# A packed attention and two MLP layers on one core: input splits made in pairs, conversions of w_in2 spread from step 46

## The chip, the cores and the metric

The kernel runs on one core of a Trainium2 chip. The time is the device time of one launch in microseconds (us), the median of several runs. The engines of the core work side by side and wait for one another by semaphores: TensorE (PE; its weight loads are listed as PEld), VectorE (DVE), ScalarE (ACT), GpSimd (POOL), and SyncE (SP), which here issues all DMA transfers in the order of the program. Every engine does its own instructions in order. The kernel fixes that order by hand.

## The reference

Eight batches of eight heads; 576 tokens, head size 64, 32 packed rows. With x the attention's output as 4608 rows of 512:

```
p_packed = softmax(p k^T / 8) v ;  a = softmax(q p_packed^T / 8) p_packed
x (4608 x 512) = a, heads side by side
h1 = x @ w_in1 (512 x 2048);  g1 = max(0.01 h1, h1);   y   = g1 @ w_out1 (2048 x 512)
h2 = y @ w_in2 (512 x 2048);  g2 = h2 * sigmoid(1.702 h2);  out = g2 @ w_out2 (2048 x 512)
```

The weights come as float64 words and are made float32 on the chip ("conversion").

## The kernel before

There are four stages. The first does attention and the product with w_in1 together and writes g1 to memory (g1_scratch, feature by token). The second, **y**, is g1 @ w_out1. The third, **h**, is y @ w_in2 with the gated activation and writes g2. The fourth, **sum**, is g2 @ w_out2. y, h and sum multiply by a scheme of seven products in place of eight for a two-by-two split of the matrices (tokens in halves i of 384, features in halves h), so their inputs need sums first. Each product is done to nearly full float32 precision with three matmuls on split inputs: an operand is a rounded high part and a remainder, and high x high, high x low and low x high are added.

y and sum have the same plan, `prepare`. The tokens are cut into 6 blocks of 768; a block has 7 products of 8 steps (`steps`: block, product p in the order 1, 7, 5, 6, 2, 4, 3, and f from 0 to 7), 56 steps in all. A step takes one 128-feature slice of an input of 384 tokens. In y it has six matmuls (L649), in sum nine (L761). Before step k, `high` (L489 and on) makes the split input: ScalarE copies 128x384 to the rounded high part (L491), and one step later VectorE subtracts it from the source to get the low part (in `split`, L107; every split of the kernel has this line). The two parts lie in a ring of ROLL = 5 slots; the copy for step k is emitted at step k - 3, the subtraction at k - 2. The copy must wait until TensorE has finished with the slot's last user, step k - 5.

The sources are `raws`, tiles of two features by 384 tokens (128x768) for the four quarters (token half, feature half), each loaded for the next block when the last reader of this one is done. Four series of sums, each of four VectorE instructions of 128x768, change them in place: S3 (L479) before product 7, S1 (L481) before product 5, S2 (L483) before product 6, S4 (L485) before product 3. After S4 the quarter (0,0) of the next block is loaded. When a product ends, `evacuate` adds or copies its bank: by ScalarE after products 1, 7 and 2 (L510, L512, L516), by VectorE after 5, 6, 4 and 3 (L514, L519, L524), with one more sum (L520) three steps after product 6 and the stores of c11, v, c10, c01.

The order is an agenda: `at(step, todo)` puts work on a step, and `side(step)` emits it ahead of that step's matmuls. `pieces` puts the parts of a generator on given steps. `combined` does so for the conversions: each of the 16 pieces of w_in2 loads its raw words at step s (L138, L139, on SP); from s + late on come ScalarE's two instructions (L121, L122), a step later VectorE's mask (L125), a step later its shift (L128) and GpSimd's add (L129), three steps on two subtractions (L144, L145), then two more (L147, L148), and the store of the seven combinations, wi_scratch (L151). The tiles raw, v and b of a conversion exist once, so the next must wait for their last use. These sixteen conversions lie among y's steps.

`y_block` makes the inputs of h the same way, for a block of y: it loads four quarters (L578), splits each of the seven products' inputs in two halves (`one`, L585 and L107), and makes sums in place between them (L591 to L596). That of block 0 lies in the last block of y, that of block 1 at h's start, and the later ones in h. Weights for h are split by `new_weights` (L625 and L107), those for sum in halves on sum's first steps (L458 and L107).

Of the kernel before, what the change touches and what calls it, by code (L numbers as in the profile page):

```python
# [9 lines left out]
F32 = mybir.dt.float32  # L10
F32R = mybir.dt.float32r
# [10 lines left out]
P = 128  # L22
# [4 lines left out]
HB = TB // 2  # L27
# [12 lines left out]
PLACE = {1: (0, 0), 7: (0, 0), 5: (1, 0), 6: (0, 0), 2: (0, 1), 4: (1, 1), 3: (0, 1)}  # L40

COMBO = {1: 0, 2: 1, 3: 2, 5: 3, 7: 4, 6: 5, 4: 6}
EARLY = 5
ROLL, LEAD = 5, 2


def packed_attention_moe_moe_kernel(tc, qT, kT, vm, vt, pT, w_in1, w_out1, w_in2, w_out2, out):
# [4 lines left out]
    nc = tc.nc  # L52
# [13 lines left out]
    pools = {}  # L66
# [13 lines left out]
    with ExitStack() as ctx:  # L80
# [10 lines left out]
        def at(step, *todo):  # L91
            agenda.setdefault(step, []).extend(todo)
# [9 lines left out]
        def split(step, high):  # L102


            rest = []
            at(step, lambda: rest.extend(high()))
            at(step + 1, lambda: nc.vector.tensor_sub(*rest))  # L107

        def pieces(piece, steps):

            for step in steps:
                at(step, lambda: next(piece, None))
# [19 lines left out]
        def combine(name, source, scratch):  # L132


            conv = pools["conv"]
            raw = conv.tile([P, 4, 256], U32, tag="raw", name=f"raw_{name}")
            for i, (x, y) in enumerate(((0, 1), (0, 0))):
                nc.sync.dma_start(raw[:, i], source[:, x, y])  # L138
            nc.sync.dma_start(raw[:, 2:4], source[:, 1])  # L139
            yield  # L140
            b = conv.tile([P, 8, P], F32, tag="b", name=f"b_{name}")
            v = conv.tile([P, 4 * P], F32, tag="v", name=f"v_{name}")
            yield from to_f32(b[:, 0:4].rearrange("p i w -> p (i w)"), raw.rearrange("p i (w t) -> p (i w) t", t=2), v, True)
            nc.vector.tensor_sub(b[:, 4], b[:, 0], b[:, 1])  # L144
            nc.vector.tensor_sub(b[:, 5], b[:, 3], b[:, 0])  # L145
            yield
            nc.vector.tensor_sub(b[:, 6], b[:, 3], b[:, 4])  # L147
            nc.vector.tensor_sub(b[:, 7], b[:, 2], b[:, 6])  # L148
            if scratch is not wo1c:
                yield  # L150
                nc.sync.dma_start(place(name, scratch), b[:, 1:8])  # L151
                return
            yield
            h = pools["px"].tile([P, 2, 7, P], F32R, tag="hl", name=f"hl_{name}")
            nc.scalar.copy(h[:, 0], b[:, 1:8])
            yield
            nc.vector.tensor_sub(h[:, 1], b[:, 1:8], h[:, 0].bitcast(F32))
            yield
            for x in range(2):
                nc.sync.dma_start(place(name, scratch)[:, x], h[:, x].bitcast(F32))  # L160
# [5 lines left out]
        def combined(what, first, late):  # L166

            view, to = {"wo1": (w_out1_v, wo1c), "wi2": (w_in2_v, wi2c), "wo2": (w_out2_v, wo2c)}[what]
            for n, s in enumerate(first):
                j, u = divmod(n, 2)  # L170
                src = view[:, :, u, :, j, :] if what == "wi2" else view[:, :, j, :, u, :]
                pieces(combine(f"{what}_{j}_{u}", src, to), (s, *(s + late + k for k in (0, 1, 2, 5, 6, 7, 8, 9))))
# [232 lines left out]
        for n in range(4, 16):  # L405
            s = 5 * (n // 4) - 5 + n % 4
# [6 lines left out]
        for b in range(B):  # L413
            s = 32 * b
# [18 lines left out]
        wt, raws, ga, outs, early = {}, {}, {}, {}, {}  # L433
# [29 lines left out]
        def load_raw(blk, i, h, fp, nm, g):  # L463
            if blk < NBK:
                home, tag = "dr", f"r{i}{h}{fp}"
                if nm == "d":
                    home, tag = ("cy", f"y{fp}") if (i, h) == (1, 0) else ("d" if h else "d0", tag)
                t = pools[home].tile([P, 2, HB], F32, tag=tag, name=f"{nm}r_{blk}_{i}{h}{fp}")
                f0, t0 = NJ * h + 2 * fp, TB * blk + HB * i
                nc.sync.dma_start(t, g[f0:f0 + 2, :, t0:t0 + HB].rearrange("f p t -> p f t"))  # L470
                raws[blk, i, h, fp] = t

        def prepare(nm, g):


            def combo(blk, fp, what):
                a11, a12, a21, a22 = (raws.get((blk, i, h, fp)) for i in range(2) for h in range(2))
                if what == "S3":
                    nc.vector.tensor_sub(a11, a11, a21)  # L479
                elif what == "S1":  # L480
                    nc.vector.tensor_add(a21, a21, a22)  # L481
                elif what == "S2":
                    nc.vector.tensor_sub(a11, a22, a11)  # L483
                else:
                    nc.vector.tensor_sub(a12, a12, a11)  # L485
                    load_raw(blk + 1, 0, 0, fp, nm, g)

            def high(k, blk, p, f):
                src = raws[(blk, *PLACE[p], f // 2)][:, f % 2, :]  # L489
                t = ga[blk, p, f] = pools["dr"].tile([P, 2, HB], F32R, tag=f"s{k % ROLL}", name=f"{nm}a_{blk}_{p}_{f}")  # L490
                nc.scalar.copy(t[:, 0, :], src)  # L491
                return t[:, 1, :], src, t[:, 0, :].bitcast(F32)

            for blk in range(NBK):
                s = 7 * NJ * blk
                for what, when in (("S3", (1, 4, 7, 10)), ("S1", (12, 14, 16, 19)), ("S2", (20, 22, 24, 27)), ("S4", (34, 38, 42, 46))):
                    for fp, k in enumerate(when):
                        at(s + k, lambda blk=blk, fp=fp, what=what: combo(blk, fp, what))
            for k, step in enumerate(steps):
                split(k - LEAD - 1, lambda k=k, step=step: high(k, *step))  # L500
                blk, p, f = step
                if f % 2 and p in (5, 4, 3):
                    at(k - LEAD, lambda blk=blk, p=p, f=f: load_raw(blk + 1, *PLACE[p], f // 2, nm, g))

        def evacuate(k, blk, p, bank, shape, store):
            def tile_(what):
# [31 lines left out]
        for k in range(EARLY):  # L538
            s = 32 * (B - 2) + 20 + 8 * k
# [29 lines left out]
        def y_block(early, steps, blk):  # L569

            t0 = TB * blk
            q = {}

            def load():
                for i, j in ((0, 0), (1, 0), (1, 1), (0, 1)):
                    home, tag = ("dr", f"r10{2 * i + j}") if blk == 0 else ("cy", f"y{2 * i + j}")
                    q[i, j] = pools[home].tile([P, 2, HB], F32, tag=tag, name=f"yq_{blk}_{i}{j}")
                    nc.sync.dma_start(q[i, j], yT[2 * j:2 * j + 2, :, t0 + HB * i:t0 + HB * i + HB].rearrange("d p t -> p d t"))  # L578

            def one(p, k):  # L580
                src, i = q[PLACE[p]], PRODUCTS.index(p)
                if blk not in ya:
                    ya[blk] = pools["ABC"[blk % 3]].tile([P, 7, 2, 2, HB], F32R, tag="ABC"[blk % 3], name=f"ya_{blk}")
                t = ya[blk][:, i]
                nc.scalar.copy(t[:, 0, k], src[:, k])  # L585
                return t[:, 1, k], src[:, k], t[:, 0, k].bitcast(F32)

            def combo(p):
                sub = nc.vector.tensor_sub
                if p == 1:  # L590
                    sub(q[0, 0], q[0, 0], q[1, 0])  # L591
                    nc.vector.tensor_add(q[1, 0], q[1, 0], q[1, 1])
                elif p == 7:
                    sub(q[0, 0], q[1, 1], q[0, 0])
                elif p == 6:
                    sub(q[0, 1], q[0, 1], q[0, 0])  # L596
            at(early, load)
            for n, step in enumerate(steps):
                p, k = (1, 2, 7, 5, 6, 4, 3)[n // 2], n % 2
                split(step, lambda p=p, k=k: one(p, k))  # L600
                if k:
                    at(step + 1, lambda p=p: combo(p))

        PIECES = (slice(0, 2), slice(2, 4), slice(4, 6), slice(6, 7))
# [27 lines left out]
        first_raws("b", g1)  # L632
        later_weights(lambda n: "w5" if n < 8 else "d", wo1c, "wo1")
        prepare("b", g1)
        combined("wi2", [26, 44] + [56 * blk + k for blk in range(1, 5) for k in (1, 19, 38)] + [281, 299], 14)
        last = 7 * NJ * (NBK - 1)
        y_block(last + 24, range(last + 28, last + 56, 2), 0)
        side_until(0)
        for k, (blk, p, f) in enumerate(steps):
# [82 lines left out]
        for q in range(2):  # L722
            s = 14 * NJ * q
# [3 lines left out]
        for k in range(EARLY):  # L727
            s = 7 * (4 * NJ + 2 * k + 2)
# [22 lines left out]
        first_raws("d", g2)  # L751
        later_weights(lambda n: "d", wo2c, "wo2")
        prepare("d", g2)
        side_until(0)
        for k, (blk, p, f) in enumerate(steps):
# [55 lines left out]
```

## Time and profile before

| | before |
|---|---|
| runs | 1472.9, 1468.38, 1469.59 us, median 1469.59 |
| the profiled execution | 1471.63 us; its span, first to last instruction, 1469.8 us |
| TensorE busy | 1403.5 us |
| VectorE, ScalarE, GpSimd busy | 1106.6, 836.6, 100.0 us |
| mean granted TensorE clock | 0.989 of full speed |
| y, from its first matmul to h's first | 352.4 to 734.3 us |
| sum, first to last matmul | 1100.5 to 1465.2 us |

A line of the profile names the place in the kernel (L649), the engine, the operation, and the tiles written and read. Tile names: br and ba are the raw and split inputs of y, dr and da those of sum, yq and ya those of h; wo and wj are weights; raw_wi, v_wi and b_wi are the tiles of a conversion of w_in2. A step of y can be told from the time, since a step's matmuls follow each other without gaps unless an engine is late.

### The profile page before, as it was taken

What the parts mean: (1) busy time and instruction counts of PE and PEld (TensorE: products, weight loads), DVE (VectorE), ACT (ScalarE), POOL (GpSimd) and SP (SyncE); (2) the same over time, 40 slices, a digit from 0 to 9 for tenths busy, and PEclk for the clock granted to TensorE, in tenths of its full rate; (3) what the DMA queues carried; (4) which work ended last, traced back from release to release, by engine and by line L of the source; (5) the groups of instructions that cost most, each with busy time, mean ns of one, the idle gap of its engine ahead of it and who ended that gap; (6) DMA issues with size and microseconds to landing.
All of it is one profiled execution on the core that took longest, in us unless ns stands there. A gap on an engine that the chain in (4) does not pass through costs nothing.

```text
span 1469.8 us, 27704 instructions
## 1 busy us (share of the span) xinstructions
PE 1403.5 (95%) x10400; PEld 1315.9 (90%) x10400; DVE 1106.6 (75%) x2068; ACT 836.6 (57%) x1791; POOL 100.0 (7%) x71
## 2 busy tenths in 40 slices
PE   6899999998999999999899999999999999999998
PEld 4577777778899999999789999999999999999998
DVE  6757677753688878888878787887558887787776
ACT  4666666755454555545566666666545555445443
POOL 1401110100011011010100000100000000000000
PEclk7999999999999999999999999999999999999999
DMA  9679999979965563655267777777667534515421
GB/s 340 227 259 331 315 315 328 298 244 340 355 205 183 179 220 98 215 180 161 85 213 276 256 254 245 246 242 249 210 230 258 172 111 142 169 55 173 137 79 44
DMA packets 228773, 317.42 MB, mean 216 GB/s; under 512 B 12576, under 2 KB 188704, under 8 KB 228640
## 3 DMA queue, kind: packets, MB, share of 16 engines
q1 hardware_dynamic: 228640, 315.67, 64.9%
q8 instruction: 81, 1.33, 0.4%
q14 instruction: 52, 0.43, 0.1%
HBM read 191.89 MB, written 123.73 MB: 215 GB/s over the span
## 4 chain that ended last, share of the span: by engine, by line
PE 69%; DVE 17%; DMA 5%; issue 3%; ACT 3%; POOL 2%; SPq 1%; DVEq 0%; ACTq 0%; POOLq 0%
PE sum L761 23%; PE h L683 19%; PE y L649 13%; PE h L338 10%; DVE ba L107 3%; PE m L218 2%; POOL b_wi L129 1%; DMA raw_wo<-in_w_out_dram 1%; PE s L218 1%; DMA br<-g_scratch 1%; DMA wo_scratch<-b_wo 1%; DMA yq<-y_scratch 1%; DVE br L481 1%; PE pp L273 1%; DVE wj L107 1%
## 5 line engine op out<-in xcount | busy, mean ns | idle before, releaser
L683 PE MATMUL h<-ya,wj 128*128 128x384 f32 x2016 | 357.8, 338 | 6.7 <-DVE uv L691 2.3
L683 PEld LDWEIGHTS h<-ya,wj 128*128 128x128 f32 x2016 | 352.6, 189 | 11.8 <-DVE uv L691 4.0
L338 PEld LDWEIGHTS h<-a,m 128*128 128x128 f32 x1536 | 209.5, 190 | 55.3 <-ACT g L343 24.9
L649 PE MATMUL y<-ba,wo 128*128 128x384 f32 x1296 | 238.7, 341 | 16.9 <-DVE ba L107 11.9
L649 PEld LDWEIGHTS y<-ba,wo 128*128 128x128 f32 x1296 | 226.4, 190 | 28.3 <-DVE ba L107 23.1
L491 ACT CAST ba<-br 128x384 fp32r<-128x384 f32 x336 | 164.5, 513 | 150.6 <-PE y L649 90.7
L491 ACT CAST da<-dr 128x384 fp32r<-128x384 f32 x336 | 166.3, 514 | 145.3 <-PE sum L761 104.2
L338 PE MATMUL h<-a,m 128*128 128x288 f32 x1536 | 232.6, 303 | 12.5 <-ACT a L315 6.4
L761 PE MATMUL sum<-wo,da 128*128 128x256 f32 x1944 | 232.5, 281 | 1.5 <-DVE da L107 1.3
L761 PEld LDWEIGHTS sum<-wo,da 128*128 128x128 f32 x1944 | 230.3, 188 | 3.2 <-DVE da L107 3.2
L107 DVE TENSOR_TENSOR da<-dr,da 128x384 fp32r<-128x384 f32 x336 | 172.5, 552 | 40.6 <-ACT da L491 40.4
L107 DVE TENSOR_TENSOR ba<-br,ba 128x384 fp32r<-128x384 f32 x336 | 175.5, 555 | 24.5 <-ACT ba L491 24.5
L343 ACT ACTIVATE g<-h 128x288 f32<-128x288 f32 x256 | 105.0, 416 | 91.8 <-PE h L338 90.3
L761 PE MATMUL sum<-wo_early,da 128*128 128x256 f32 x1080 | 132.4, 285 | 1.7 <-ACT da L491 1.6
L761 PEld LDWEIGHTS sum<-wo_early,da 128*128 128x128 f32 x1080 | 131.5, 193 | 2.2 <-ACT da L491 1.9
L649 PE MATMUL y<-ba,wo_early 128*128 128x384 f32 x720 | 126.9, 337 | 4.1 <-ACT ba L491 2.7
L649 PEld LDWEIGHTS y<-ba,wo_early 128*128 128x128 f32 x720 | 124.7, 188 | 5.4 <-ACT ba L491 3.0
L327 DVE TENSOR_TENSOR m<-m,m 128x512 fp32r<-128x512 f32 x64 | 43.0, 683 | 46.9 <-ACT m L325 45.8
L129 POOL TENSOR_TENSOR b_wo<-v_wo,b_wo 128x512 int32<-128x512 int32 x32 | 42.6, 1331 | 485.4 <-DVE v_wo L128 381.0
L676 ACT ACTIVATE g<-cc 128x384 f32<-128x384 f32 x96 | 50.4, 525 | 31.8 <-DVE cc L699 27.3
L107 DVE TENSOR_TENSOR wj<-wjs,wj 128x512 fp32r<-128x512 f32 x88 | 55.8, 646 | 9.2 <-ACT wj L625 9.1
L691 DVE TENSOR_TENSOR uv<-uv,h 128x384 f32<-128x384 f32 x48 | 26.5, 553 | 47.5 <-PE h L683 40.9
(114 smaller groups left out, 1362.8 us busy)
## 6 DMA issues: line engine op xcount, KB each, us to landing
g_scratch<-g SPq DMA_DIRECT2D x64, 576.0 KB, 5.5
br<-g_scratch SPq DMA_DIRECT2D x96, 384.0 KB, 6.6
g_scratch<-g SPq DMA_DIRECT2D x96, 384.0 KB, 5.0
dr<-g_scratch SPq DMA_DIRECT2D x96, 384.0 KB, 4.6
wjs<-wi_scratch SPq DMA_DIRECT2D x22, 896.0 KB, 5.7
wo_scratch<-hl_wo SPq DMA_DIRECT2D x32, 448.0 KB, 5.9
wo<-wo_scratch SPq DMA_DIRECT2D x27, 512.0 KB, 8.9
k<-in_kT_dram SPq DMA_DIRECT2D x16, 576.0 KB, 7.4
```

The source lines that it names most:

```text
L107: at(step + 1, lambda: nc.vector.tensor_sub(*rest))
L129: nc.gpsimd.tensor_tensor(d, v.bitcast(I32), d, op=ALU.add)
L218: nc.tensor.matmul(tiles[par][32 * i:32 * i + 32, :n], lhsT=lhsT(r, i, par), rhs=rhs(r, i), start=True, stop=True)
L327: nc.vector.tensor_sub(m[:, 1, par, :], t[par], m[:, 0, par, :].bitcast(F32))
L338: nc.tensor.matmul(t[:, :TH], lhsT=m[:, ws, par, o:o + P], rhs=a[:, xs, par, :], start=(k == 0), stop=(k == 5))
L343: nc.scalar.activation(g1t[g][:, f % 2, hf * TH:hf * TH + TH], t[:, :TH], AF.Prelu, alpha=0.01)
L491: nc.scalar.copy(t[:, 0, :], src)
L649: nc.tensor.matmul(acc[BANK[p]][:, c, :HB], lhsT=w[:, ws, P * c:P * c + P], rhs=x[:, xs, :], start=(p in OPENS and f + m == 0), stop=(f == ...
L676: nc.scalar.activation(g[f][:, HB * i:HB * i + HB], src, AF.Gelu_apprx_sigmoid)
L683: nc.tensor.matmul(b, lhsT=w[:, ws, c, P * kk:P * kk + P], rhs=x[:, xs, kk, :], start=(p in OPENS and kk + s == 0), stop=(kk + s == 3), sk ...
L691: nc.vector.tensor_add(v, v, b)
L761: nc.tensor.matmul(b, lhsT=x[:, xs, P * c:P * c + P], rhs=w[:, ws, :], start=(p in OPENS and f == 0 and m == 0 and c != 1), stop=(f == NJ ...
```

## The change

Three things change. The split in `high` and the one in `one` are made for two slices at once (128x768), so there are half as many; the ring has three slots of two slices each, and the copy for a pair (k, k + 1) is emitted at step k - 4, the subtraction at k - 3. The sums S3, S1 and S2 are emitted every two steps from step 1 to 23 of a block (before, 1 to 27), S4 at 36 to 43 (before, 34 to 46). The sixteen conversions of w_in2 start at steps 46, 61, ... 271, each 15 after the one before, their compute part 11 steps later (before, they started at 26, 44, then at 1, 19 and 38 of blocks 1 to 4, then at 281 and 299, the compute part 14 steps later).

```diff
-ROLL, LEAD = 5, 2
+ROLL = 3
...
             def high(k, blk, p, f):
-                src = raws[(blk, *PLACE[p], f // 2)][:, f % 2, :]
-                t = ga[blk, p, f] = pools["dr"].tile([P, 2, HB], F32R, tag=f"s{k % ROLL}", name=f"{nm}a_{blk}_{p}_{f}")
-                nc.scalar.copy(t[:, 0, :], src)
-                return t[:, 1, :], src, t[:, 0, :].bitcast(F32)
+                src = raws[(blk, *PLACE[p], f // 2)]
+                t = pools["dr"].tile([P, 2, 2, HB], F32R, tag=f"s{k // 2 % ROLL}", name=f"{nm}a_{blk}_{p}_{f}")
+                for c in range(2):
+                    ga[blk, p, f + c] = t[:, :, c]
+                nc.scalar.copy(t[:, 0], src)
+                return t[:, 1], src, t[:, 0].bitcast(F32)
...
-                for what, when in (("S3", (1, 4, 7, 10)), ("S1", (12, 14, 16, 19)), ("S2", (20, 22, 24, 27)), ("S4", (34, 38, 42, 46))):
+                for what, when in (("S3", (1, 3, 5, 7)), ("S1", (9, 11, 13, 15)), ("S2", (17, 19, 21, 23)), ("S4", (36, 39, 41, 43))):
...
             for k, step in enumerate(steps):
-                split(k - LEAD - 1, lambda k=k, step=step: high(k, *step))
                 blk, p, f = step
-                if f % 2 and p in (5, 4, 3):
-                    at(k - LEAD, lambda blk=blk, p=p, f=f: load_raw(blk + 1, *PLACE[p], f // 2, nm, g))
+                if f % 2 == 0:
+                    split(k - 4, lambda k=k, step=step: high(k, *step))
+                elif p in (5, 4, 3):
+                    at(k - 2, lambda blk=blk, p=p, f=f: load_raw(blk + 1, *PLACE[p], f // 2, nm, g))
...
-            def one(p, k):
+            def one(p):
...
-                nc.scalar.copy(t[:, 0, k], src[:, k])
-                return t[:, 1, k], src[:, k], t[:, 0, k].bitcast(F32)
+                nc.scalar.copy(t[:, 0], src)
+                return t[:, 1], src, t[:, 0].bitcast(F32)
...
             for n, step in enumerate(steps):
-                p, k = (1, 2, 7, 5, 6, 4, 3)[n // 2], n % 2
-                split(step, lambda p=p, k=k: one(p, k))
-                if k:
+                if n % 2 == 0:
+                    p = (1, 2, 7, 5, 6, 4, 3)[n // 2]
+                    split(step, lambda p=p: one(p))
                     at(step + 1, lambda p=p: combo(p))
...
-        combined("wi2", [26, 44] + [56 * blk + k for blk in range(1, 5) for k in (1, 19, 38)] + [281, 299], 14)
+        combined("wi2", range(46, 46 + 16 * 15, 15), 11)
```

## Rows read from the trace of the kernel before

**Rows 1.** The page: busy time, share of the span and instructions of each engine.
```profile
PE 1403.5 (95%) x10400; PEld 1315.9 (90%) x10400; DVE 1106.6 (75%) x2068; ACT 836.6 (57%) x1791; POOL 100.0 (7%) x71
```
**Rows 2.** Busy us (and count) of PE, PEld, DVE, ACT, POOL; clock; DMA share, GB/s.
```profile
352.40:421.90 69.50, 62.38 (x337) 60.92 (x338) 48.76 (x84) 31.87 (x64) 1.43 (x1) 0.95 1.04 351
421.90:483.60 61.70, 60.10 (x337) 57.96 (x336) 52.94 (x97) 33.57 (x67) 9.55 (x4) 1.00 0.54 173
...
544.60:605.60 61.00, 59.79 (x338) 58.19 (x338) 52.05 (x95) 32.79 (x65) 6.26 (x3) 1.00 0.55 177
...
666.60:734.50 67.90, 61.95 (x338) 57.85 (x337) 62.20 (x113) 37.06 (x77) 5.70 (x2) 1.00 0.33 103
1100.50:1164.30 63.80, 62.37 (x504) 61.56 (x505) 56.30 (x96) 39.46 (x80) 0.00 (x0) 0.97 0.76 249
1164.30:1224.20 59.90, 59.86 (x506) 59.66 (x505) 45.52 (x77) 29.85 (x59) 0.00 (x0) 1.00 0.42 133
```
**Rows 3.** Instructions in order of time, block 3 of y: start, us, engine, line, count.
```profile
544.61 20.97 PE L649 MATMUL y<-ba,wo_early 128*128 128x384 f32 x120
```
**Rows 4.** Waits within y: who for whom, us in total, times, longest.
```profile
PE y L649 <- DVE ba L107: 13.3, 24, 1.4
PE y L649 <- ACT ba L491: 7.4, 2, 4.7
```
**Rows 5.** Order of time, block 0 of y (in brackets: idle before, releaser).
```profile
357.60 17.78 PE L649 MATMUL y<-ba,wo_early 128*128 128x384 f32 x101 [1.21 <-DVE ba L107]
...
392.75 1.58 SPq L449 DMA_DIRECT2D wo<-wo_scratch  x1
394.38 2.55 SPq L138 DMA_DIRECT2D raw_wi<-in_w_in_dram  x2
...
403.77 0.66 ACT L121 ACTIVATE b_wi<-raw_wi 128x512 int32<-128x512 uint32 x1 [5.91 <-DMA raw_wi<-in_w_in_dram]
```
**Rows 6.** Busy times around the stop in block 0, columns as in rows 2.
```profile
398.00:414.00 16.00, 10.38 (x43) 9.81 (x43) 8.24 (x16) 5.05 (x11) 1.43 (x1) 0.79 0.98 327
406.00:410.00 4.00, 3.17 (x10) 3.17 (x11) 4.00 (x8) 1.54 (x4) 1.43 (x1) 0.50 0.95 300
```
**Rows 7.** Order of time, block 3 of y, columns as in rows 3 and 5.
```profile
564.00 1.48 POOL L129 TENSOR_TENSOR b_wi<-v_wi,b_wi 128x512 int32<-128x512 int32 x1 [19.53 <-DVE v_wi L128]
564.25 2.05 DVE L481 TENSOR_TENSOR br<-br,br 128x768 f32<-128x768 f32 x1
...
573.56 1.68 PE L649 MATMUL y<-ba,wo 128*128 128x384 f32 x8 [0.32 <-DVE ba L107]
...
589.02 0.29 DVE L144 TENSOR_TENSOR b_wi<-b_wi 128x128 f32<-128x128 f32 x1 [1.19 <-POOL b_wi L129]
...
597.46 0.95 DVE L524 TENSOR_TENSOR c<-u,y 128x768 f32<-128x768 f32 x1 [1.46 <-PE y L649]
598.33 2.43 DVE L107 TENSOR_TENSOR ba<-br,ba 128x384 fp32r<-128x384 f32 x5
```
**Rows 8.** Order of time on TensorE, block 5 of y and h's first block.
```profile
715.36 1.32 PE L649 MATMUL y<-ba,wo 128*128 128x384 f32 x6 [1.42 <-DVE ba L107]
...
759.10 0.81 PE L683 MATMUL h<-ya,wj 128*128 128x384 f32 x3 [1.62 <-DVE ya L107]
```
**Rows 9.** Groups of instructions: busy us, mean ns of one, idle before, releasers.
```profile
L107 DVE TENSOR_TENSOR ba<-br,ba 128x384 fp32r<-128x384 f32 x336 | 175.5, 555 | 24.5 <-ACT ba L491 24.5
L491 ACT CAST ba<-br 128x384 fp32r<-128x384 f32 x336 | 164.5, 513 | 150.6 <-PE y L649 90.7 <-DVE br L481 25.0 <-DVE br L483 22.6
L157 DVE TENSOR_TENSOR hl_wo<-b_wo,hl_wo 128x896 fp32r<-128x896 f32 x16 | 17.3, 1081 | 6.7 <-ACT hl_wo L155 5.4 <-DMA raw_wo<-in_w_out_dram 1.1
L155 ACT CAST hl_wo<-b_wo 128x896 fp32r<-128x896 f32 x16 | 15.1, 945 | 8.9 <-DVE b_wo L148 8.6 <-issue 0.3
```
**Rows 10.** The tile b_wi: its stores, from issue to landing.
```profile
DMA to landing us min/median/max: 3.3/6.4/8.2
```
**Rows 11.** DMA issues from 345 to 425: count, KB each, median us to landing.
```profile
wo<-wo_scratch SPq DMA_DIRECT2D x18, 512.0 KB, 9.1
```

## The prediction

> **What bounds the kernel now.** The page first: TensorE 95% busy, VectorE 75%, ScalarE 57% [rows 1]. A share over the span doesn't say what a stage loses, so the busy times by stage came next, cut at the block borders of the wide products y and sum [rows 2]. What a block must take follows from one undisturbed run of matmuls in y: 120 within 20.97 us, one lasting 0.34, so they start (20.97 - 0.34) / 119 = 0.1734 us apart; a step (six) is 1.04 us, a block (56 steps) 58.25 us [rows 3]. The y blocks took 69.5, 61.7, three times 61.0, and 67.9: lost are 11.2 + 3.5 + 3 x 2.75 + 9.7 = 32.7 us. In sum a block takes 59.9 at its best (a step 1.07); its first, 63.8, loses 3.9, the others together about 1.5. So the matter is y.
>
> The waits inside y say who makes TensorE late: VectorE's subtraction L107, 13.3 us in 24 waits, and twice ScalarE's copy, 7.4 us, the longer 4.7 [rows 4].
>
> The last view is the order of time, in three places. In block 0 ScalarE stands 5.91 us at the first conversion of w_in2 (L121), whose raw words are only asked for at 394.38, behind the weight loads; the copies queue behind it [rows 5]. From 398 to 414 TensorE starts 43 matmuls where 92 fit, 49 x 0.1734 = 8.5 us lost, part of it at half clock: granted were 0.50 (1.2 of 2.4 GHz) at 406 to 410, after the stop [rows 6]. Another 1.9 went at the entry: the 20th matmul started at 357.60 where 352.4 + 19 x 0.1734 = 355.7 was possible [rows 2, 5]. In a middle block TensorE waits for L107 around step 24, where the sums S1 and S2 stand one step before the copies that read them, with a conversion between them, and again after L144, which itself waits 1.19 for GpSimd [rows 7]. Block 5 has such waits of up to 1.42, with y's own splits, weights and a conversion in one place [rows 8].
>
> **The change, part by part.**
> *Pairs.* VectorE does 384 columns back to back in (2.43 - 0.55) / 4 = 0.47 us; a 768-wide instruction is followed 0.87 later (597.46 to 598.33) [rows 7]. Two become one: 0.94 to 0.87, 28 x 0.07 = 2.0 us per block. No split of 768 stands in the trace; between 384 (0.555) and 896 (1.081) it comes to 0.95 on VectorE, and between 0.513 and 0.945 to 0.84 on ScalarE [rows 9], two copies of 0.51 becoming one, beside TensorE. But a pair's low half is ready 0.84 + 0.95 = 1.79 after its copy starts, where 0.51 + 0.55 = 1.06 did: 0.73 later. The slot comes free at the start of step k - 4 in both kernels, so of 4 x 1.04 = 4.16 us the first half keeps some 2.2 of slack (with 0.1 for each handover) where it had 2.9; the second has 1.04 more. At the entry of y and of sum the first matmul comes 0.33 later and the low half up to 0.73, but then one split serves two steps; I take -0.4 at each (bounds -1 and +0.7).
> Here a rule speaks against the change. VectorE is busy 52.05 us of a 61.0 us block, not full, and yet TensorE waits for it [rows 2, 4]. The Trainium skill, Perfetto Trace Analysis, "Optimizing Scalar/DVE Operations", says that grouping helps a saturated engine, and that where ScalarE or VectorE aren't saturated but cause bubbles elsewhere, breaking instructions up may complete work sooner. By the rule the pairs go the wrong way and the time would be rival B's, 1486.7, instead of 1439.9.
>
> *Sums ahead.* VectorE's emitted order becomes, every two steps up to 23, one sum and one pair: 2 x 0.87 = 1.74 of 2.08 us, and each sum now stands three steps before the copy that reads it. A subtraction behind an evacuation that waits for TensorE (L514, L519, L524) used to be two steps ahead of its use; now it is for a pair at least three steps ahead: evacuation 0.95, subtraction 0.95 and handovers end some 2.1 us into 4.16. So the waits around step 24 lose both causes. What is late next is a conversion in the dense part. Its VectorE work is 0.33 + 0.6 + 4 x 0.21 = 1.8 us start to start, plus about 1.15, paid either by a sum that takes 2.05 instead of 0.95 beside GpSimd's add (564.00) or by the wait at L144 [rows 7]; 2.95 in all. Against it stand the slack of 2.2 and 0.34 regained per pair, 0.85 over the five steps it takes: 3.05. It just fits; where two conversions fall into the first 26 steps (blocks 1 and 2) a few tenths may show.
> In demand VectorE gains nothing. Before: 56 x 0.47 + 16 sums x 0.87 + 5 evacuations x 0.87 + 3 conversions x 2.95 = 53.4 us a block. After: 28 x 0.87 + 13.9 + 4.35 + 3.73 (one in 15 steps) x 2.95 = 53.6, of 58.25. The gain must come from order alone. I take 0.4 us lost in each of blocks 1 to 4 (bounds 0 and the old 2.75): -3.1 and 3 x -2.35, together -10.1.
>
> *Conversions from step 46.* Block 0 keeps only one raw load of them. It leaves at step 46, ScalarE wants it at 57. The weight load issued at 392.75 lands 9.1 later, near 402 [rows 5, 11]; ahead of the raw words then stand the store of v, four loads of (0,0), the store of c11 and four of (1,1), ten transfers of 384 KB, 3.93 MB at the 350 GB/s or so of this stretch (327 with the stop in it [rows 6]): 11.2 us, and 1.5 for themselves, 414.7. Step 57 comes at 352.4 + 1.5 + 59.3 = 413.2. L121 may wait 1.5, inside the slack. I take 2.0 lost in block 0 (entry 1.5, 0.5 elsewhere) instead of 11.2: -9.2 (bounds -0.5, the old stop kept, and -11).
> The other queues: SP loses the two old loads from the crowd before 402, and a later raw load waits only for L128 of the conversion before, two steps earlier in the order; behind it on SP are the loads of the next block's inputs, which have ten steps and more to spare. What gets tighter is the tile b: its store is issued at s + 18 and the next L121 comes at s + 26, 8 steps later (before, 11 or more). The store lands 3.3 to 8.2 us after issue, median 6.4 [rows 10]; issued 3.2 us after the start of step s + 17, it lands in the median 9.6 us after that start, step 26 comes at 9.4. So that wait is 0.2 in the median and 2.0 at the longest, with all of ScalarE's copies behind it. I take nothing for it, and keep it as rival C.
> In block 5 the conversion in the crowded half goes (the last one stands at steps 3 to 9 there). VectorE's demand in steps 28 to 55 was 28 x 0.47 + 4 sums 3.5 + 14 splits of y x 0.47 + 4 sums of y 3.5 + 3 evacuations 2.6 + weights 2.2 + conversion 2.95 = 34.5 in 28 x 1.04 = 29.1 us, 5.4 too many (that half lost some 7). After: 14 x 0.87 + 3.5 + 7 x 0.87 + 3.5 + 2.6 + 2.2 = 30.1, 1.0 too many. I take 2.4 lost in the block instead of 9.7: -7.3 (bounds -3 and -9.5).
>
> *h and sum.* In h's first block 14 splits become 7 pairs, 6.6 to 6.1 us of VectorE, where TensorE waits up to 1.62 for it [rows 8]: -0.5 (bounds -3 and +1.5). In sum there is no conversion; the 0.3 a block goes with the order (-1.5), block 0 gives 0.7 of what it loses where weight halves crowd, the entry 0.4: -2.6 (bounds -4.5 and +2). y's entry is in block 0's term.
>
> **Sum.** -9.2 - 10.1 - 7.3 - 0.5 - 2.6 = -29.7. The profiled execution took 1471.6 (span 1469.8): 1441.9. It is 2.0 above the median of the runs shown, so 1439.9 against 1469.6, -2.0%.
>
> **The rivals.**
> A, the peaks stay: demand is 53.6 against 53.4, and more conversions fall among the sums. Then blocks 1 to 4 keep their losses; block 0 gains 8.5, block 5 5.0, sum 1.0: -14.5, 1455.1. For it: the unchanged demand. Against: sum, with the same sums and no conversion, loses only 0.3 a block.
> B, slower: pairs are ready 0.73 later at every place where VectorE is late now. Five waits in each of blocks 1 to 4 and seven in block 5 grow by it, 27 x 0.73 = 19.7; two in each block of sum, 8.8. Block 0 still gives 8.5 and block 5's conversion 2.95: +17.1, 1486.7. It decides once a sum, an evacuation or a conversion holds a pair's subtraction back by more than 2.2 us as a rule. Against it: the waits stand where order made VectorE late, not length. The Trainium skill's rule above would make this the outcome.
> C, the tile b: with the longest landing the loop of a conversion (6 steps, 2.5 us of lateness, 0.7 to issue, 8.2 to land) is 17.6 us against 15 steps = 15.6. 15 x 2.0 = 30 eats the gain: 1469.9. Against: a store that leaves in a quiet stretch lands in 3.3, and the slack takes one such wait.
> D, the first raw words come 4 us or more after 414.7 and block 0 keeps its stop: 1448.4.
>
> **How the numbers follow.** Forecast 0.68, A 0.15, B 0.04, C 0.05, D 0.08. The forecast's own spread is 1433 to 1447, from the bounds of blocks 0 and 5 and of h; the range goes on over D and A, 1433 to 1456, and leaves out B and C (0.09) and about 0.05 on either side. A measurement of this kernel tells about 0.3% (4.4 us) from no change. Forecast, A and D are faster by more, 0.91, and C in a milder form 0.02: 0.93. Same 0.03 (C), slower 0.04 (B).
>
> **What would show it.** Right: y blocks 1 to 4 near 58.6, block 0 near 60, block 5 near 60.6; no wait of ScalarE for the raw words over 2 us; a clock of 1.00 at 400 to 420; splits of 128x768 at about 0.95 on VectorE and 0.84 on ScalarE; L121 without a wait for the store of b. Wrong: blocks of 61 us, with L144 standing before TensorE's waits (A); more waits for L107 than before, spread over the block (B); ScalarE's idle time in front of L121 put down to the store (C). A split much longer than 0.95 would upset the whole sum.

## The result and the profile after

The changed kernel takes 1445.57 us (median; 1444.15 to 1447.15) against 1470.03 for the kernel before beside it (1468.38 to 1472.9): ratio 0.9832, 95% interval 0.9811 to 0.9852, 24.5 us less. The profiled execution took 1444.28, its span 1442.5 (before 1469.8).

Busy us and count of PE, PEld, DVE, ACT, POOL, then clock, DMA share and GB/s, of the changed kernel: the six blocks of y, then the first two of sum.

```profile
354.30:413.70 59.40, 58.83 (x337) 58.41 (x338) 45.41 (x50) 26.37 (x32) 0.00 (x0) 1.00 1.07 364
413.70:473.40 59.70, 59.30 (x338) 58.06 (x337) 54.91 (x73) 29.98 (x39) 7.50 (x4) 1.00 0.64 205
473.40:532.90 59.50, 59.01 (x337) 58.05 (x336) 53.41 (x69) 30.08 (x39) 7.53 (x4) 1.00 0.62 201
532.90:591.60 58.70, 58.70 (x338) 58.15 (x337) 53.19 (x72) 29.86 (x39) 5.66 (x3) 1.00 0.62 197
591.60:651.30 59.70, 59.22 (x339) 58.14 (x338) 52.84 (x73) 29.17 (x38) 7.82 (x4) 1.00 0.63 204
651.30:712.40 61.10, 59.46 (x338) 58.28 (x338) 56.30 (x68) 31.88 (x42) 1.88 (x1) 1.00 0.24 81
1076.90:1138.40 61.50, 61.27 (x504) 60.97 (x505) 55.10 (x68) 35.41 (x50) 0.00 (x0) 0.97 0.77 257
1138.40:1198.50 60.10, 60.10 (x507) 60.10 (x506) 44.70 (x49) 25.50 (x31) 0.00 (x0) 1.00 0.42 132
```

Against [rows 2], y's blocks went from 69.5, 61.7, 61.0, 61.0, 61.0, 67.9 to 59.4, 59.7, 59.5, 58.7, 59.7, 61.1: -24.0 in all. VectorE's busy time in a middle block rose by 1 us and more (52.05 to 53.19 and 53.41) while the block got shorter. Part of it is no work: instructions that stand still beside GpSimd's add (shown below) make up 1.1 us of a middle block before and 2.7 to 3.7 after. Without them VectorE's work fell by 0.5 to 1.2 us a block, so this table can't tell order from work; the runs below can. The third column from the right shows the clock at 1.00 through block 0.

The waits of TensorE within y, in us, times and longest, answer to [rows 4]; the 2.6 is the stage's entry.

```profile
PE y L652 <- DVE ba L107: 3.6, 7, 1.2
PE y L652 <- ACT ba L493: 2.6, 1, 2.6
```

Stage by stage (from each stage's first matmul to the next stage's, sum to its last) y went from 381.9 to 357.9 us, h from 366.1 to 364.6, sum from 364.7 to 361.0: -29.2. The first stage, which the change doesn't touch, took 1.9 longer in this execution, so the span fell by 27.3. The medians fell by 24.5 only, because the profiled execution before lay 1.6 above its median and the one after 1.3 below. Over the 13 profiled executions told of here y's first matmul comes anywhere from 352.0 to 358.4 us, and nothing that was changed explains the order.

What still makes TensorE late in a middle block stands in order of time (block 1, steps 20 to 22; VectorE, GpSimd and TensorE):

```profile
434.21 0.70 DVE L128 SCALAR_TENSOR_TENSOR v_wi<-v_wi,raw_wi 128x512 uint32<-128x512 uint32 x1
434.82 0.95 DVE L483 TENSOR_TENSOR br<-br,br 128x768 f32<-128x768 f32 x1
435.04 1.89 POOL L129 TENSOR_TENSOR b_wi<-v_wi,b_wi 128x512 int32<-128x512 int32 x1 [13.58 <-DVE v_wi L128]
435.69 2.06 DVE L107 TENSOR_TENSOR ba<-br,ba 128x768 fp32r<-128x768 f32 x1
437.80 8.50 PE L652 MATMUL y<-ba,wo 128*128 128x384 f32 x46 [0.39 <-DVE ba L107]
```

The sum that began before GpSimd's add takes its 0.95; the next instruction, a split, takes 2.06. The add ends at 436.93 and the split at 437.75, 0.82 later, so it stood still until the add was done. TensorE waits for that split. Fourteen of the sixteen conversions hold a split in this way, ten of them for 1.1 us, but not every held split makes TensorE late. Behind each of the seven at steps 2 to 24 of a block, among the sums S3, S1 and S2, the gaps between matmuls come to about 0.2 to 1.0 us; behind the seven at steps 28 to 53 there are none.

### The profile page after: what moved, and what is told of

It reads as the page before. It is cut to its first block, busy times and chain, and to the rows that moved or that the text cites. A ratio compares the mean times of both kernels' runs of the same rounds, so it can differ in the third digit from the quotient of the medians.

```text
span 1442.5 us, 26605 instructions
## 1 busy us (share of the span) xinstructions
PE 1393.5 (97%) x10400; PEld 1314.5 (91%) x10400; DVE 1091.9 (76%) x1690; ACT 784.4 (54%) x1413; POOL 94.6 (7%) x71
## 5 line engine op out<-in xcount | busy, mean ns | idle before, releaser
L493 ACT CAST da<-dr 128x768 fp32r<-128x768 f32 x168 | 140.2, 836 | 171.2 <-PE sum L764 156.3
L652 PE MATMUL y<-ba,wo 128*128 128x384 f32 x1296 | 227.7, 336 | 2.2 <-DVE ba L107 2.2
L493 ACT CAST ba<-br 128x768 fp32r<-128x768 f32 x168 | 140.6, 837 | 155.6 <-PE y L652 131.8
L107 DVE TENSOR_TENSOR da<-dr,da 128x768 fp32r<-128x768 f32 x168 | 160.5, 956 | 75.3 <-ACT da L493 74.2
L107 DVE TENSOR_TENSOR ba<-br,ba 128x768 fp32r<-128x768 f32 x168 | 172.9, 1032 | 41.0 <-ACT ba L493 39.7
```

What stands on the lines that cost most here:

```text
L493: nc.scalar.copy(t[:, 0], src)
L652: nc.tensor.matmul(acc[BANK[p]][:, c, :HB], lhsT=w[:, ws, P * c:P * c + P], rhs=x[:, xs, :], start=(p in OPENS and f + m == 0), stop=(f == ...
```

## The experiments

The change has three parts: pairs, sums ahead, conversions from step 46. The first five of the runs below are parts of it alone and in twos (pairs with the conversions, without the sums ahead, was not run); the ratios are to the kernel before, with 95% intervals.

**Pairs alone.** The new `high` and `one`, with

```diff
-("S1", (9, 11, 13, 15)), ("S2", (17, 19, 21, 23))
+("S1", (12, 14, 16, 18)), ("S2", (20, 22, 24, 26))
-combined("wi2", range(46, 46 + 16 * 15, 15), 11)
+combined("wi2", [26, 44] + [56 * blk + k for blk in range(1, 5) for k in (1, 19, 38)] + [281, 299], 14)
```

(S3 and S4 as before, too.)

> Pairs alone: splits of 128x768 with the ring of three pairs, in y, sum and y_block; conversions where they were before, sums where they were before except that the last of S1 and of S2 stands one step earlier (18, 26), as the pair's copy needs. Theory (order made VectorE late; a pair's subtraction stands three to four steps ahead and so outlives an evacuation): the waits behind evacuations go, those in front of tight sums stay, block 0 keeps its stop of 8.5 us: about 1463 us, -7, of which sum gives 3. Rival (the length of a pair costs: 0.73 us more at every wait): slower than before by 5 us or more, with longer waits for L107 in blocks 1 to 4 than 2.75 us a block.

1520.65 us, ratio 1.0327 (1.0303 to 1.0352): 48 us slower, in every block of both products but y's first (69.5 to 67.6, where the first raw words came without a wait). So my reason for the pairs was not enough by itself, and the rival had the sign, though not the way. In order of time, block 1 of sum, with no conversion anywhere near:

```profile
1203.43 0.95 DVE L481 TENSOR_TENSOR dr<-dr,dr 128x768 f32<-128x768 f32 x1
1204.50 0.83 ACT L493 CAST da<-dr 128x768 fp32r<-128x768 f32 x1 [1.97 <-DVE dr L481]
1205.36 0.96 DVE L107 TENSOR_TENSOR da<-dr,da 128x768 fp32r<-128x768 f32 x1 [0.98 <-ACT da L493]
1206.24 0.95 DVE L481 TENSOR_TENSOR dr<-dr,dr 128x768 f32<-128x768 f32 x1
1207.30 0.84 ACT L493 CAST da<-dr 128x768 fp32r<-128x768 f32 x1 [1.97 <-DVE dr L481]
...
1208.17 0.96 DVE L107 TENSOR_TENSOR da<-dr,da 128x768 fp32r<-128x768 f32 x1 [0.98 <-ACT da L493]
```

A sum now stands at the step of its copy, behind the subtraction of the pair before. VectorE and ScalarE take turns: sum, copy, subtraction, next sum. Copy to copy is 1207.30 - 1204.50 = 2.80 us, where two steps of sum are 2.14. Eight pairs per block (S1 and S2) losing 0.66 each would be 5.3 us; sum's blocks took 64.8 instead of 59.9, y's middle blocks 65.4 instead of 61.0 (windows of that run):

```profile
552.60:618.00 65.40, 61.05 (x339) 58.00 (x338) 50.09 (x68) 28.71 (x37) 6.59 (x4) 1.00 0.52 168
1189.40:1254.20 64.80, 61.76 (x506) 60.12 (x506) 44.72 (x49) 25.27 (x31) 0.00 (x0) 1.00 0.39 124
```

VectorE is busy 44.72 of 64.80 us there: a chain, not a full engine.

**Sums ahead alone.**

```diff
-(("S3", (1, 4, 7, 10)), ("S1", (12, 14, 16, 19)), ("S2", (20, 22, 24, 27)), ("S4", (34, 38, 42, 46)))
+(("S3", (1, 3, 5, 7)), ("S1", (9, 11, 13, 15)), ("S2", (17, 19, 21, 23)), ("S4", (36, 39, 41, 43)))
```

> Sums ahead alone (1 to 7, 9 to 15, 17 to 23, 36 to 43), single splits in the ring of five, conversions where they were. Theory: each sum stands three steps before its copy, the waits around step 24 shrink by about 1.5 us in five blocks, sum's by 1: about 1461 us, -9; the stop in block 0 stays. Rival (the lead of the pairs does it, not the place of the sums): the subtraction behind an evacuation is still two steps ahead, and no more than 3 us are gained.

1468.15 us, ratio 0.9978 (0.9963 to 0.9994), about 3 us: nearer the rival. Sum gave 2.9 us, y's middle blocks only 0.3 each (61.0 to 60.7): TensorE's waits there still lie at steps 5, 21 to 26 and 41, behind the adds of the conversions at steps 54, 18 and 36.

**Conversions alone.**

```diff
-combined("wi2", [26, 44] + [56 * blk + k for blk in range(1, 5) for k in (1, 19, 38)] + [281, 299], 14)
+combined("wi2", range(46, 46 + 16 * 15, 15), 11)
```

> Conversions of w_in2 at 46, 61, ... 271 with 11 steps to the compute part, all else as before. Theory: block 0's stop of 8.5 us goes and block 5 loses one conversion of 2.95 us in its crowded half and some of its queue (-5), while blocks 1 to 4 have 3.7 conversions in place of 3 among tight sums (+0.5 to +1 each): about 1459 us, -11. Rival (the store of b, or the raw words at step 57): ScalarE waits in front of L121 for 2 us and more at several conversions, and the gain stays under 5 us.

1463.29 us, ratio 0.9938 (0.9916 to 0.9961), about -9: block 0 fell from 69.5 to 60.7 us, block 5 from 67.9 to 63.1, and blocks 1 to 4 took 63.8, 59.3, 62.1, 62.3, together 2.8 more than before. As the theory had it. The rival's wait was there, but small: in front of L121 ScalarE idled 3.3 us in all y, 1.8 of it for the store of b.

**Sums ahead and conversions, no pairs** (both diffs above on the kernel before).

> Sums ahead and conversions from step 46 with 11 steps, but single splits in the ring of five: the change without the pairs. Theory (a pair's worth is its lead of three to four steps, as its subtraction outlives an evacuation and a conversion): block 0's stop is gone as with the conversions alone, blocks 1 to 4 lose about 1.5 to 2 us each where a conversion meets the sums, sum is near 361: about 1457 us, 11 above the changed kernel. Rival (the sums and the conversions did it all): within 3 us of the changed kernel.

1457.9 us, ratio 0.9916 (0.9900 to 0.9933): what the two gave alone, and the pairs are worth 12 us on top of them.

**Pairs and sums ahead, old conversions** (the changed kernel with its last diff line undone).

> Pairs and sums ahead, conversions where they were before (26, 44, ... with 14 steps): the change without its third part. Theory: the chain that slowed the pairs alone (sum, copy, subtraction, next sum one after the other) is gone since a sum now stands three steps before its copy; sum as in the changed kernel; block 0 keeps its stop of about 8.5 us and block 5 its conversion (3 us): about 1457 us. Rival (pairs cost by themselves, 0.73 us at each wait): waits of 0.7 us every two steps as with the pairs alone, over 1480 us.

1455.78 us, ratio 0.9899 (0.9881 to 0.9917). The same pairs that cost 48 us alone gain 12 here. Block 0 keeps its stop; a middle block takes 58.4 us, less than in the changed kernel. ScalarE in block 0, then a middle block's window, answer to [rows 5] and [rows 2]:

```profile
406.76 0.66 ACT L121 ACTIVATE b_wi<-raw_wi 128x512 int32<-128x512 uint32 x1 [6.99 <-DMA raw_wi<-in_w_in_dram]
```
```profile
542.70:601.10 58.40, 58.40 (x337) 58.17 (x337) 51.65 (x68) 28.96 (x37) 5.63 (x4) 1.00 0.58 188
```

So the third part is worth 10 us (1455.8 to 1445.6) by blocks 0 (69.4 to 59.4) and 5 (66.0 to 61.1), and gives some back in between.

These middle blocks also show that a held split need not cost anything. In each of blocks 2 to 4 two splits stand still beside GpSimd's add, at steps 19 and 37, and TensorE goes on (block 3, step 19; later in the block it loses 0.1 us):

```profile
562.59 0.95 DVE L483 TENSOR_TENSOR br<-br,br 128x768 f32<-128x768 f32 x1
562.81 1.89 POOL L129 TENSOR_TENSOR b_wi<-v_wi,b_wi 128x512 int32<-128x512 int32 x1 [18.88 <-DVE v_wi L128]
563.46 2.06 DVE L107 TENSOR_TENSOR ba<-br,ba 128x768 fp32r<-128x768 f32 x1
563.51 3.28 PE L652 MATMUL y<-ba,wo 128*128 128x384 f32 x18
```

**The lead without the width.** The kernel with sums and conversions and

```diff
-ROLL, LEAD = 5, 2
+ROLL, LEAD = 6, 3
```

> Sums ahead and conversions as in the changed kernel, single splits, but a ring of six slots with the copy four steps and the subtraction three steps ahead: the lead and the room of the pairs without their width. Theory (the lead is what the pairs give): within 4 us of the changed kernel, 1442 to 1449. Rival (fewer, wider instructions are what they give): near the kernel with the ring of five, 1455 or more.

1450.86 us, ratio 0.9865 (0.9847 to 0.9882): between the two. Of the 12 us that pairs add to sums and conversions, 7 come with a ring of six and one step more of lead, in single splits; about 5 are left for the width, an estimate from medians whose intervals overlap a little (0.9847 to 0.9852). This run undoes the pairs in y_block too: in the profiled executions y took 3.6 us longer than in the changed kernel and h 1.3.

**One step ahead.**

```diff
-(("S3", (1, 3, 5, 7)), ("S1", (9, 11, 13, 15)), ("S2", (17, 19, 21, 23)), ...
+(("S3", (3, 5, 7, 9)), ("S1", (11, 13, 15, 17)), ("S2", (19, 21, 23, 25)), ...
```

> The changed kernel with S3, S1 and S2 two steps later (3 to 9, 11 to 17, 19 to 25): each sum now stands one step before the copy that reads it, but still ahead of the subtraction of the pair before. With the pairs alone a sum stood at the step of its copy, behind that subtraction, and y and sum lost 0.7 us every two steps from 18 to 30. Theory (there VectorE and ScalarE worked one after the other: sum, copy, subtraction, and only then the next sum, 0.95 + 0.84 + 0.95 us and handovers against 2.08): one place in the order is enough, sum stays near 361 us and the time within 3 us of the changed kernel. Rival (the distance of three steps is needed): sum's blocks go to 61 us and more, the time to 1455 or more.

1444.37 us, ratio 0.9809 (0.9786 to 0.9831): no slower than the changed kernel. A sum two steps later, but emitted ahead of the earlier pair's subtraction, is enough, and a block of sum takes 59.6 (block 2, with the columns of the windows above):

```profile
1195.50:1255.10 59.60, 59.60 (x506) 59.60 (x505) 44.82 (x49) 25.48 (x31) 0.00 (x0) 1.00 0.42 133
```

In sum, which has no conversions, this and the pairs alone differ in that S1 and S2 come one step earlier, and in the places of S3 and S4. The waits of the pairs alone lie at S1 and S2, so nearly all of the 5 us per block is that one place in VectorE's order.

**Without GpSimd's add in w_in2's conversions.**

```diff
-nc.vector.tensor_scalar(hi, hi, 0x80000000, None, op0=ALU.bitwise_and)
-nc.vector.scalar_tensor_tensor(v, v, 3, hi, op0=ALU.logical_shift_left, op1=ALU.bitwise_or)
-nc.gpsimd.tensor_tensor(d, v.bitcast(I32), d, op=ALU.add)
+nc.vector.scalar_tensor_tensor(hi, hi, 0x80000000, d, op0=ALU.bitwise_and, op1=ALU.bitwise_or)
+nc.vector.scalar_tensor_tensor(d, v, 3, hi, op0=ALU.logical_shift_left, op1=ALU.bitwise_or)
```

(ScalarE's scale for d is 0.936 of what it was, so that d rounds to 0 to 7.)

> The changed kernel with GpSimd's add taken out of the sixteen conversions of w_in2: VectorE joins the low bits by two bit operations (the mask L125 becomes mask-and-or, 0.43 to about 0.68 us, and the shift writes b directly); the low three bits are rounded a little differently. In the changed kernel blocks 1 to 4 still lose 1.2 us each. Theory (while GpSimd adds, the next VectorE instruction with two inputs stands still, and now that is a split, 2.05 in place of 0.95 us): all splits are near 0.95, blocks 1 to 4 come to 58.7, about 4 us less than the changed kernel, 1441. Rival (VectorE's demand of 53.6 of 58.25 us, or the distance from the copy, is what is left): splits become equal but blocks 1 to 4 stay above 59.2 and less than 1.5 us is gained.

1440.4 us, ratio 0.9788 (0.9764 to 0.9813). The splits of y (busy, mean ns, idle before), first in the changed kernel, then without the add, and its blocks 1 to 4:

```profile
L107 DVE TENSOR_TENSOR ba<-br,ba 128x768 fp32r<-128x768 f32 x168 | 172.9, 1032 | 41.0 <-ACT ba L493 39.7 <-DMA raw_wi<-in_w_in_dram 1.1
```
```profile
L107 DVE TENSOR_TENSOR ba<-br,ba 128x768 fp32r<-128x768 f32 x168 | 160.2, 955 | 45.4 <-ACT ba L500 45.2
```
```profile
412.00:470.60 58.60, 58.60 (x337) 58.11 (x337) 52.13 (x73) 30.00 (x39) 0.00 (x0) 1.00 0.66 218
470.60:528.90 58.30, 58.30 (x338) 58.30 (x338) 51.73 (x70) 30.12 (x39) 0.00 (x0) 1.00 0.61 198
528.90:587.10 58.20, 58.20 (x337) 58.20 (x336) 51.16 (x71) 29.68 (x39) 0.00 (x0) 1.00 0.63 199
587.10:645.80 58.70, 58.70 (x339) 58.26 (x338) 52.12 (x73) 29.28 (x38) 0.00 (x0) 1.00 0.64 206
```

168 x (1032 - 955) = 12.9 us of standing still are gone, and with them nearly all that blocks 1 to 4 lost: they take 58.2 to 58.7 where 58.25 is what the matmuls need. So GpSimd's add is the cause of what they lost, though most of the 12.9 us cost TensorE nothing. A second run of the same kernel, for its spread:

> A second look at the changed kernel without GpSimd's add in the conversions of w_in2, for its spread: blocks 1 to 4 of y between 58.2 and 58.8 us again, the time within 1438 to 1444.

1440.65 us in one run, and blocks 1 to 4 took 58.3 to 58.8. y took 354.8 us there, 353.6 in the first: block 0 had 60.6 us at a granted clock of 0.97, in the first 59.3 at 1.00.

**y's block 1 later in h.**

```diff
-y_block(-1, range(4, 18), 1)
+y_block(-1, range(6, 20), 1)
```

> The changed kernel with the splits of y's block 1 in h started two steps later (6 to 18 instead of 4 to 16). In h's first block the changed kernel loses 6.3 us at steps 7 to 9, where the kernel before lost 2.0, and 1.4 at step 20, where it lost 4.5: two sums of y now stand ahead of the split of the second weights. Theory: with the sums behind it the loss at steps 7 to 9 falls to about 2.5, step 20 loses up to 1 more, the time falls by 2 to 4 us. Rival (the weights' own DMA, which lands late, sets these steps): no change.

1445.63 us, ratio 0.982 (0.9796 to 0.9844): no change, the theory missed. TensorE at h's start, the changed kernel and then this one:

```profile
725.63 14.20 PE L686 MATMUL h<-ya,wj 128*128 128x384 f32 x71 [2.58 <-DVE wj L107]
```
```profile
722.69 8.56 PE L686 MATMUL h<-ya,wj 128*128 128x384 f32 x47 [0.32 <-DVE wj L107]
731.93 3.67 PE L686 MATMUL h<-ya,wj 128*128 128x384 f32 x18 [0.68 <-DVE ya L107]
737.42 2.19 PE L686 MATMUL h<-ya,wj 128*128 128x384 f32 x6 [1.82 <-DVE ya L107]
```

The wait for the weights fell from 2.58 to 0.32 us and came back at steps 16 to 21 as waits for y's own splits. VectorE is busy 13.6 of the 14.0 us from 720 to 734 in this run, but only 15.8 of h's first 23 us in the changed kernel, so a full VectorE doesn't explain both. In both the granted clock adds to the loss: its mean behind the waits was 0.80 from 726 to 733 us in the changed kernel and 0.75 from 734 to 741 here. Why the two orders lose about the same isn't shown.

**No add in the conversions of w_out1, w_in2 and w_out2, and y's block 1 later.** The diff without the add for all conversions that `combine` makes, with the one above. The 16 conversions of w_in1 don't go through `combine` and keep GpSimd's add, other than the expectation says.

> The changed kernel with GpSimd's add taken out of all conversions (w_in1, w_out1, w_in2, w_out2; the low three bits joined by VectorE's bit operations, rounded a little differently) and y's block 1 two steps later in h. Theory: blocks 1 to 4 of y at 58.2 to 58.7 us as without the add in w_in2 alone, some tenths to 2 us less in the first stage and h where GpSimd's add also stands beside VectorE, h's start 2 to 4 us less: 1434 to 1438. Rival (VectorE's longer mask, 0.25 us in 64 conversions, costs in the first stage, whose order is tight): 1441 or more.

1438.72 us, ratio 0.977 (0.9746 to 0.9794): the fastest median, 0.7 above the theory's range, but its interval overlaps that of the version with w_in2's conversions alone (0.9764 to 0.9813), so a gain over that one isn't shown. Blocks 1 to 4 took 58.3 to 58.4 as the theory had it; h took 364.1, 0.5 less than in the changed kernel and not 2 to 4. Block 0 took 62.4 in this execution, at a granted clock of 0.95.

## Why the prediction was right

The time, 1445.6, lies in the range, 5.7 above the point. By the traces the five terms sum to -29.2 where I had -29.7. The rest of the distance is the first stage's 1.9 in the profiled execution, the 1.3 by which the median lies above that execution, and the 2.0 that I took off because the profiled execution before lay above its median. That the sum agrees to 0.5 is in part luck: blocks 1 to 4 gave 3.0 less than forecast, and block 0, h and sum together 3.0 more.

- *Block 0*, -9.2 forecast: 69.5 to 59.4, -10.1. The clock stayed at 1.00. The first raw words were late as reckoned, and by less: ScalarE stood 0.70 us for them at step 57, where I had up to 1.5.
- *Blocks 1 to 4*, -10.1: 2.0 + 1.5 + 2.3 + 1.3 = -7.1. This is the mis-sized term. The step that failed is "It just fits", 2.95 against 3.05 of slack. The blocks lost 1.45, 1.25, 0.45 and 1.45 us instead of 0.4. Taking GpSimd's add away showed that they lost it to the add: they took 58.2 to 58.7 then. I had let the add hold a sum, or the wait at L144; in the changed order it mostly holds a split, and by the trace 2.95 fits at some places and not at others. TensorE lost about 1.0 us behind the one at step 2 of block 4 (0.35 of it also without the add), 0.9 behind step 20 of block 1 and 0.2 behind step 13 of block 3. My "few tenths" for two conversions in the first 26 steps points the right way (blocks 1, 2 and 4 have two, block 3 one), but in block 4 most of the loss already lies behind the first.
- *Block 5*, -7.3: 67.9 to 61.1, -6.8. *h*, -0.5: -1.5 (its matmuls -1.8, sum's entry +0.3), but not where I put it, so its size is luck. h's first 56 steps, for which I had reckoned the term, took 1.3 longer (65.6 to 66.9): most of the waits at steps 19 to 21 [rows 8] went and larger ones came at 7 to 9. The third and the fifth 56 steps took 2.8 and 1.5 less. *Sum*, -2.6: -3.7, -2.3 of it in its first block, where I had 0.7; no step is late after its first two.
- *The pair's cost*: 0.955 and 0.84 us as interpolated, where GpSimd doesn't hold it.
- *Demand equal, order decides*: order is borne out, and more strongly than I said: the pairs alone keep VectorE busy for 50.1 us of a middle block, less than before, and take 4.4 us longer. I weighed a pair's lead against its length, but not what a pair does to sums that stand where they stood: the loop of 2.80 us. The three parts don't add (alone +48, -3, -9; together -24.5), because the pairs need the sums ahead; my forecast for the pairs alone, -7, was wrong by 55.
- *Rival A* (peaks stay) is right in part: about four tenths stayed (4.6 of 11.8 us), where A put them, at conversions among the sums, but with one wait at L144 only. *Rival B* describes the pairs alone by sign. The Trainium skill's rule (Perfetto Trace Analysis, "Optimizing Scalar/DVE Operations"), that where ScalarE and VectorE aren't saturated but cause bubbles on other engines, breaking instructions up may complete work sooner, agrees with that run, 1520.65 against 1472.34 beside it. With the sums ahead the same pairs gain 12 us, so the rule did not decide this change. *Rival C*: the store of b landed in 3.3 to 7.8 us, median 3.6, not 6.4, and one L121 waited 1.0 for it. *Rival D* did not come: 0.70.

What stays open: which part of the width's 5 us is VectorE's and which ScalarE's, why TensorE loses 0.9 us behind a held split at one step among the sums and 0.1 at another, what sets the loss at h's start, and why the first stage varies by 6 us between executions.

## What to carry to other kernels

When two in-order engines hand work to each other, look for the loop (sum, copy, subtraction, next sum) before counting their busy time: an instruction one place too late in one queue cost 0.66 us a pair with VectorE 69% busy, and one place earlier it cost nothing. Merging small instructions cost 48 us here with that loop and gained 12 once it was cut, more of it by room and lead (7) than by width (5). What can hold a queue (a DMA not yet landed, another engine's add) belongs where the queue has slack: here TensorE lost up to 0.9 us behind a held split among the sums, and nothing behind one after them.

## What the hardware showed that was not expected

While GpSimd adds two tiles, a VectorE instruction with two inputs can stand still: 2.05 to 2.06 us in place of 0.95, with the add at 1.48 to 1.89 us [rows 7]. It isn't always VectorE that is held. In the same changed kernel one add took 2.75 us while a sum and a split beside it took their 0.95, and then the subtraction at L144 waited for the add:

```profile
610.51 0.95 DVE L483 TENSOR_TENSOR br<-br,br 128x768 f32<-128x768 f32 x1
610.72 2.75 POOL L129 TENSOR_TENSOR b_wi<-v_wi,b_wi 128x512 int32<-128x512 int32 x1 [14.98 <-DVE v_wi L128]
611.38 0.95 DVE L107 TENSOR_TENSOR ba<-br,ba 128x768 fp32r<-128x768 f32 x1
613.50 0.29 DVE L144 TENSOR_TENSOR b_wi<-b_wi 128x128 f32<-128x128 f32 x1 [1.18 <-POOL b_wi L129]
```

I had seen both in the trace before and not asked which it would be after the change. Joining the same bits on VectorE alone, with a mask of 0.69 us instead of 0.43, made y 4.3 us shorter (357.9 to 353.6).
